# Sparse attention and a dense layer on one core: own keys, summaries and edge keys in one 128-row block

## The chip, the cores and the metric

The kernel runs on one core of a Trainium2 chip. The core has TensorE (matrix products, PE in the profile; its weight loads are PEld), VectorE (DVE), ScalarE (ACT), GpSimd (POOL) and SyncE (SP), with an on-chip memory of 128 partitions (SBUF) and a smaller accumulator memory (PSUM, eight banks of 2 KB per partition) that TensorE writes. DMA queues bring data from memory. The metric is the device time of one execution in microseconds.

## The reference

Two layers. The first is attention with 4 batches, 8 heads, 768 positions and 64 dimensions. Each query sees the keys less than 16 positions away, and one summary for each of 24 blocks of 32 keys: the maximum of the block's keys as key, the mean of its values as value, with log 32 added to the score. The second is a dense layer, 512 to 2048 to 512, with the gate h * clip(h + 3, 0, 6) / 6 between.

```python
k_sum = k.reshape(B, H, nb, block, D).max(axis=3)
v_sum = v.reshape(B, H, nb, block, D).mean(axis=3)
scores_l = scale * np.matmul(q, k.transpose(0, 1, 3, 2))
mask_l = np.abs(pos[:, None] - pos[None, :]) < window
scores_s = scale * np.einsum('bhsd,bhnd->bhsn', q, k_sum) + np.log(block)
scores_all = np.concatenate([np.where(mask_l, scores_l, -1e9), scores_s], axis=-1)
a = softmax(scores_all)
attn = np.matmul(a, np.concatenate([v, v_sum], axis=2))
x = attn.transpose(0, 2, 1, 3).reshape(B * S, H * D)
h = x @ w_in
out = (h * np.clip(h + 3.0, 0.0, 6.0) / 6.0) @ w_out
```

## The kernel before

Heads are taken in pairs p = 0 to 3, so that two heads of 64 dimensions fill 128 partitions. For each batch b and pair p:

- Tk (L264) transposes k by TensorE into PSUM. Copies put the two heads into `kbd[p]`, block-diagonal by blocks of 64 keys (L281, L283). A reduction takes the maximum of each 32 keys (L285, L287), and a product puts it into `kst[p]` (L292, L296). Tq (L298) transposes q and one copy puts it into `qT[p]`.
- Sl (L316) makes local scores by key blocks: for each block of 64 keys of both heads a matmul against the 94 queries in reach (L321), then the exponential (L324) and the product with a band mask (L325), into `at[p]`. Ss (L327) makes summary scores for two pairs at once, 96 rows, with an exponential of its own (L334) into `asum`.
- AV (L348) makes, for half of the positions, the numerator: one matmul of the summaries with `vst` (L357) and seven of local blocks with `vbd` (L359), added up in one bank; and the denominator by five matmuls with ones (L363 to L373). 1/den comes from a logarithm and an exponential (L375, L376), and x = num/den is written by VectorE (L377).

v comes twice: as blocks into `vbd` (block-diagonal, by load_v, or for batch 0 as float32 by load_vf and casts) and as rows (load_vrows) for the sums over 32 values, which vsum (L229) makes by six additions on VectorE; for batch 0 they come from TensorE (vsum0, L247).

The dense layer runs over eight stages t of 384 positions (two per batch). F1(t, ft) makes 128 of 2048 hidden columns: four matmuls (L389), the relu on ScalarE (L392), the gate product g on VectorE (L393). F2 adds 48 matmuls into three banks for three output tiles (L402); ScalarE copies each (L406) and SP stores it (L408).

The order. All engines run their instructions in program order, each its own list. Up to line 448 the order of TensorE, ScalarE and VectorE is written by hand: batch 0's attention for the first half of its positions. After it a work list of ten rows of 16 steps interleaves F1(t) with F2(t-1): first F1(0) alone, then F1(1) with F2(0), F2(1) alone, F1(2) alone, and from there F1(t) with F2(t-1). The attention of the batches is put at numbered steps ("slots", 16 to a row) between them, and a scheduler then settles each engine's order. GpSimd's order is the program's: it issues all loads, on one queue, and with hold_loads (L488) it waits for a gate product of step 11 before the loads of batch 1. Loads of later batches are placed at slots too, where their buffers are free.

Of the kernel before, what the change touches and what calls it, by code (L numbers as in the profile page):

```python
# [9 lines left out]
F32 = mybir.dt.float32  # L10
# [6 lines left out]
D = 64  # L17
BLK = 32
KB = 64
HALO = 15  # L20
WIN = KB + 2 * HALO
HALF = 384
NLONG = 2
RUN = 8
PCS = 4
RP = 96
QCUT = 480
# [3 lines left out]
def kernel(  # L31
# [13 lines left out]
    NT = S // 128  # L45
    NK = S // KB
# [8 lines left out]
    ld = ctx.enter_context(tc.tile_pool(name="ld", bufs=4))  # L55
    work = ctx.enter_context(tc.tile_pool(name="work", bufs=2))
    xp = ctx.enter_context(tc.tile_pool(name="xp", bufs=4))
# [11 lines left out]
    kbd = [const.tile([128, NK, 128], BF16, tag=f"kbd{p}", name=f"kbd{p}") for p in range(NP)]  # L69
    vall = const.tile([128, NP, NK, 128], BF16, tag="vbd", name="vbd")  # L70
    vbd = [vall[:, p] for p in range(NP)]
    qT = [const.tile([128, S + 2 * HALO + 2], BF16, tag=f"qT{p}", name=f"qT{p}") for p in range(NP)]
    at = [const.tile([128, NK, WIN], BF16, tag=f"at{p}", name=f"at{p}") for p in range(NP)]
    kst = [const.tile([128, RS], BF16, tag=f"kst{p}", name=f"kst{p}") for p in range(NP)]
    vst = [const.tile([RS, 2, D], BF16, tag=f"vst{p}", name=f"vst{p}") for p in range(NP)]
    w_in_sb = const.tile([128, NP, d_ff], BF16, tag="win", name="win")
    w_out_sb = const.tile([128, NFT, d_model], BF16, tag="wout", name="wout")


    kb_t, qb_t, vr_t, vf = {}, {}, {}, {}  # L80

    def load_k(b, p, n=1):

        if b < NLONG:
            t = ld.tile([RP, 2 * n, RUN, D], BF16, tag=f"kb{n}", name="kb", bufs=2)
            nc.gpsimd.dma_start(out=t[:], in_=k[b, 2 * p:2 * p + 2 * n].rearrange("h (p s) d -> p h s d", s=RUN))
        else:
            t = ld.tile([128, NT, 2, D], BF16, tag="kb", name="kb")
            load_natural(t, k, b, p)
        for i in range(n):  # L90
            kb_t[b, p + i] = t, i

    def load_q(b, p, n=1, part=None):

        if b < NLONG:
            lo, hi, r = cut(part)
            t = ld.tile([(hi - lo) // r, 2 * n, r, D], BF16, tag=f"qb{n}", name="qb", bufs=1 if n == 4 else 2)
            nc.gpsimd.dma_start(
                out=t[:], in_=q[b, 2 * p:2 * p + 2 * n, lo:hi].rearrange("h (p s) d -> p h s d", s=r))
        else:  # L100
            t = ld.tile([128, NT, 2, D], BF16, tag="qb", name="qb")
            load_natural(t, q, b, p)
        for i in range(n):
            qb_t[b, p + i, part] = t, i

    def cut(part):
        return {None: (0, S, RUN), 0: (0, QCUT, RUN // 2), 1: (QCUT, S, RUN // 2)}[part]

    def load_natural(t, src, b, p):
        for j in range(2):  # L110
            nc.gpsimd.dma_start(out=t[:, :, j], in_=src[b, 2 * p + j].rearrange("(s p) d -> p s d", p=128))  # L111

    def load_v(b, g, lo=0, hi=NK):

        for p in (2 * g, 2 * g + 1):
            for j in range(2):
                rows = slice(64 * j, 64 * j + 64)
                nc.gpsimd.dma_start(out=vall[rows, p, lo:hi, rows],  # L118
                                    in_=v[b, 2 * p + j].rearrange("(n k) d -> k n d", k=KB)[:, lo:hi])

    def load_vf(p):

        if not vf:
            t = gp.tile([128, NP, NK, D], F32, tag="g", name="vf")
            vf.update({i: t[:, i] for i in range(NP)})
        for j in range(2):
            nc.gpsimd.dma_start(out=vf[p][64 * j:64 * j + 64],  # L127
                                in_=v[0, 2 * p + j].rearrange("(n k) d -> k n d", k=KB))

    def load_vrows(b, g):  # L130

        w = BLK // PCS * D
        vr_t[b, g] = ld.tile([RS, PCS, w + 8], F32, tag="vr", name="vr", bufs=2)
        nc.gpsimd.dma_start(out=vr_t[b, g][:, :, 0:w],
                            in_=v[b, 4 * g:4 * g + 4].rearrange("h (n c t) d -> (h n) c (t d)", c=PCS, n=NB))
# [11 lines left out]


    ctx.enter_context(tc.manual_schedule(engines={ET.Pool}))
    start = tc.manual_schedule(engines={ET.PE, ET.Activation, ET.DVE})  # L150
    start.__enter__()
    load_vf(0)
# [4 lines left out]
    load_vf(1)  # L157
    load_k(0, 0)
    load_q(0, 0, 1, 0)
    load_vf(2)  # L160


    mask = const.tile([128, WIN], BF16, tag="mask", name="mask")
    nc.gpsimd.memset(mask[:], 1.0)
    for j in range(2):
        m = mask[j * 64:(j + 1) * 64]
        nc.gpsimd.affine_select(out=m, in_=m, compare_op=ALU.is_ge, fill=0.0, base=0,
                                channel_multiplier=-1, pattern=[[1, WIN]])
        nc.gpsimd.affine_select(out=m, in_=m, compare_op=ALU.is_ge, fill=0.0, base=2 * HALO,
                                channel_multiplier=1, pattern=[[-1, WIN]])  # L170
    load_vf(3)
    load_k(0, 1)
    load_q(0, 1, 1, 0)
    load_k(0, 2, 2)
    load_q(0, 2, 2, 0)


    hm4 = const.tile([RS, 4, D], F32, tag="hm4", name="hm4")
    osum4 = const.tile([RS, 4, D], BF16, tag="osum4", name="osum4")
    nc.gpsimd.memset(hm4[:], 1.0)  # L180
    nc.gpsimd.affine_select(out=hm4[:], in_=hm4[:], compare_op=ALU.is_ge, fill=0.0, base=0,
                            channel_multiplier=1, pattern=[[-NB, 4], [0, D]])
    nc.gpsimd.affine_select(out=hm4[:], in_=hm4[:], compare_op=ALU.is_ge, fill=0.0, base=NB - 1,
                            channel_multiplier=-1, pattern=[[NB, 4], [0, D]])
    hmv = [hm4[:, 2 * par:2 * par + 2] for par in range(2)]
    osum = [osum4[:, 2 * par:2 * par + 2] for par in range(2)]
    obd = const.tile([128, 2, D], BF16, tag="obd", name="obd")
    hmk = const.tile([128, 2, NB], BF16, tag="hmk", name="hmk")
    half_c = const.tile([128, 1], F32, tag="half", name="half_c")
    zero = const.tile([128, 1], F32, tag="zero", name="zero")  # L190
    nc.vector.memset(zero[:], 0.0)

    def zero_off_diagonal(eng, t):
        w = t.rearrange("p n c -> p (n c)").bitcast(F32).rearrange("p (n c) -> p n c", c=64)
        for r, c in ((slice(0, 64), slice(32, 64)), (slice(64, 128), slice(0, 32))):
            if eng is nc.scalar:
                eng.copy(w[r, :, c], zero[r].unsqueeze(2).to_broadcast([64, NK, 32]))
            else:
                eng.memset(w[r, :, c], 0.0)


    ind = const.tile([128, 2, 2, 4], F32, tag="ind", name="ind")
    nc.vector.memset(ind[:], 0.0)
    for i in range(4):
        for par in range(2):
            nc.vector.memset(ind[32 * i:32 * i + 32, par, par, i:i + 1], 1.0)
    for p in range(NP):
        zero_off_diagonal(nc.vector if p < 2 else nc.scalar, kbd[p][:])
# [336 lines left out]
```

## Time and profile before

| | us |
|---|---|
| Median of 3 runs | 265.46 |
| Lowest and highest | 264.72, 266.41 |
| The profiled execution's own span | 262.8 |
| TensorE busy (1848 matmuls) | 238.0 |
| ScalarE busy | 169.3 |
| VectorE busy | 154.2 |
| GpSimd busy (104 instructions) | 72.5 |
| F1 matmuls L389 (512) | 104.1 |
| F2 matmuls L402 (360 of 384 recorded) | 96.2 |

The span runs from the first to the last instruction of one execution. Matmuls overlap in the records, each being listed with the time until its end, so the cost of a run of them is read from the start of one to the start of the next. The page gives busy shares in 40 slices of the span, a chain of waits followed back from the end, and the costliest groups of instructions. The DMA row is the busy share of 16 DMA engines in tenths, and GB/s counts the bytes that are written; weights, q and k are read as float32 and written as bfloat16.

### The profile page before, as it was taken

To read this page: it belongs to the slowest core of one execution; us is meant where nothing else is said; L and a number is where in the kernel's file an instruction comes from. 1 tells how busy PE (TensorE), PEld (TensorE's weight loads), DVE (VectorE), ACT (ScalarE), POOL (GpSimd) and SP (SyncE) were. 2 spreads that over 40 slices of the span, in tenths; PEclk is the share of its full clock that TensorE was granted. 3 is DMA by queue.
4 is the path that set the end of the run, shared out by engine and by line. 5 is a ranking of instruction groups with operands and counts; after the bars stand their busy time and mean duration, and the time that the engine had idled before them with its cause. 6 is when DMAs were issued, how large, how long until landed. Compare 5 with 4: busy or idle time off the path is not lost.

```text
span 262.8 us, 4842 instructions
## 1 busy us (share of the span) xinstructions
PE 238.0 (91%) x1848; PEld 135.9 (52%) x1872; DVE 154.2 (59%) x360; ACT 169.3 (64%) x327; POOL 72.5 (28%) x104
## 2 busy tenths in 40 slices
PE   0946899999899969999899999999999999999993
PEld 0215556644455636666455556566655555555541
DVE  3594556632889774998994566668534544444400
ACT  7665578842587867998586567757766555555410
POOL 8994000566273600796920310000000000000000
PEclk9995599999999999999999999999999999999999
DMA  3999994299999971899990551001011111101122
GB/s 111 178 155 201 206 206 76 37 204 209 203 255 118 180 80 44 58 130 187 185 145 19 54 70 44 36 7 40 2 40 40 42 40 40 40 2 41 40 82 80
DMA packets 57848, 25.80 MB, mean 98 GB/s; under 512 B 45281, under 2 KB 53217, under 8 KB 57825
## 3 DMA queue, kind: packets, MB, share of 16 engines
q0 software_dynamic: 54160, 19.14, 63.5%
q1 hardware_dynamic: 3664, 6.34, 6.5%
q8 instruction: 15, 0.25, 0.4%
q14 instruction: 9, 0.07, 0.1%
HBM read 31.98 MB, written 6.29 MB: 146 GB/s over the span
## 4 chain that ended last, share of the span: by engine, by line
PE 62%; DMA 11%; DVE 8%; ACT 7%; POOL 7%; issue 3%; ACTq 0%; POOLq 0%
PE op L402 24%; PE hp L389 24%; DMA vr<-in_v_dram 8%; POOL vbd L118 3%; PE num L359 2%; DMA vs<-vs 2%; PE sl L321 2%; POOL vf L127 2%; DVE g L393 2%; PE num L357 2%; PE ss L331 2%; ACT kbd L281 2%; PE den L363 1%; PE den L366 1%; DMA vf<-in_v_dram 1%
## 5 line engine op out<-in xcount | busy, mean ns | idle before, releaser
L389 PE MATMUL hp<-x,win 128*128 128x384 bf16 x512 | 104.1, 326 | 2.8 <-DVE g L393 2.4
L392 ACT ACTIVATE r<-hp,half_c 128x384 f32<-128x384 f32 x128 | 73.5, 580 | 45.8 <-PE hp L389 45.0
L402 PE MATMUL op<-wout,g 128*128 128x512 bf16 x360 | 96.2, 379 | 1.1 <-issue 0.2
L393 DVE SCALAR_TENSOR_TENSOR g<-r,hp 128x384 bf16<-128x384 f32 x128 | 69.6, 551 | 45.6 <-ACT r L392 45.4
L389 PEld LDWEIGHTS <-win 128*128 128x128 bf16 x512 | 47.3, 98 | 37.2 <-issue 6.0
L402 PEld LDWEIGHTS <-g 128*128 128x128 bf16 x384 | 36.8, 98 | 32.8 <-issue 0.5
L377 DVE TENSOR_TENSOR x<-num,lg 128x384 bf16<-128x384 f32 x32 | 17.7, 555 | 24.7 <-ACT lg L376 22.8
L118 POOL DMA_DIRECT2D vbd<-in_v_dram x24 | 18.2, 775 | 37.7 <-PE num L359 33.6
L375 ACT ACTIVATE lg<-den 128x384 f32<-128x384 f32 x32 | 15.7, 492 | 16.0 <-PE den L373 7.4
L324 ACT ACTIVATE at<-sl 128x376 bf16<-128x376 f32 (+2 forms) x48 | 22.4, 490 | 2.3 <-PE sl L321 2.3
L406 ACT COPY ot<-op 128x512 f32<-128x512 f32 x24 | 13.9, 583 | 8.9 <-PE op L402 8.8
L325 DVE TENSOR_TENSOR at<-at,mask 128x376 bf16<-128x376 bf16 (+2 forms) x48 | 16.2, 349 | 3.6 <-ACT at L324 3.4
L359 PEld LDWEIGHTS <-vbd 128*128 128x128 bf16 x224 | 13.8, 102 | 8.0 <-issue 4.5
L376 ACT ACTIVATE lg<-lg 128x384 f32<-128x384 f32 x32 | 16.8, 526 | 0.8
L321 PE MATMUL sl<-qT,kbd 128*128 128x94 bf16 x192 | 15.0, 214 | 1.9 <-ACT at L324 0.8
L321 PEld LDWEIGHTS <-kbd 128*128 128x128 bf16 x192 | 12.2, 102 | 7.7 <-issue 1.8
L359 PE MATMUL num<-at,vbd 128*128 128x94 bf16 (+2 forms) x224 | 15.0, 206 | 0.0
L111 POOL DMA_DIRECT2D qb<-in_q_dram x16 | 13.5, 861 | 4.8 <-DMA vr<-in_v_dram 4.8
L252 PE MATMUL vps<-vf,ind 128*8 128x384 f32 x16 | 7.5, 612 | 7.6 <-DMA vf<-in_v_dram 7.6
L111 POOL DMA_DIRECT2D kb<-in_k_dram x16 | 13.5, 865 | 0.0
L357 PE MATMUL num<-asum,vst 96*128 96x384 bf16 x32 | 11.0, 344 | 2.6 <-DVE x L377 2.2
L281 ACT COPY kbd<-tp 64x768 bf16<-64x768 bf16 x12 | 9.5, 792 | 5.2 <-PE tp L271 5.1
(82 smaller groups left out, 219.8 us busy)
## 6 DMA issues: line engine op xcount, KB each, us to landing
out_dram<-ot SPq DMA_DIRECT2D x24, 256.0 KB, 2.0
vr<-in_v_dram POOLq DMA_DIRECT2D x6, 768.0 KB, 7.7
vbd<-in_v_dram POOLq DMA_DIRECT2D x24, 96.0 KB, 3.9
win<-in_moe_w_in_dram POOLq DMA_DIRECT2D x4, 512.0 KB, 11.1
wout<-in_moe_w_out_dram POOLq DMA_DIRECT2D x4, 512.0 KB, 18.3
vf<-in_v_dram POOLq DMA_DIRECT2D x8, 192.0 KB, 3.7
kb<-in_k_dram POOLq DMA_DIRECT2D x16, 96.0 KB, 6.8
qb<-in_q_dram POOLq DMA_DIRECT2D x16, 96.0 KB, 6.4
```

What stands on the lines that cost most here:

```text
L111: nc.gpsimd.dma_start(out=t[:, :, j], in_=src[b, 2 * p + j].rearrange("(s p) d -> p s d", p=128))
L118: nc.gpsimd.dma_start(out=vall[rows, p, lo:hi, rows], in_=v[b, 2 * p + j].rearrange("(n k) d -> k n d", k=KB)[:, lo:hi])
L321: nc.tensor.matmul(sp[:, i * WIN:(i + 1) * WIN], kbd[p][:, t], qT[p][:, t * KB:t * KB + WIN], start=True, stop=True)
L324: nc.scalar.activation(a, sp[:, 0:n * WIN].rearrange("p (n c) -> p n c", c=WIN), AF.Exp, scale=scl)
L357: nc.tensor.matmul(num[:], vst[p][:].rearrange("p h d -> p (h d)"), asm[:], start=True, stop=False)
L359: nc.tensor.matmul(num[:, lo:hi], vbd[p][:, t], a[:, t, off:off + hi - lo], start=False, stop=(i == len(bl) - 1))
L376: nc.scalar.activation(lg[:], lg[:], AF.Exp, scale=-1.0)
L377: nc.vector.tensor_tensor(xt[s][:, p], num[:], lg[:], op=ALU.mult)
L389: nc.tensor.matmul(hp[:], w_in_sb[:, kt, ft * 128:(ft + 1) * 128], xt[t][:, kt], start=(kt == 0), stop=(kt == NP - 1))
L392: nc.scalar.activation(r[:], hp[:], AF.Relu, bias=half_c[:], scale=1.0 / 6.0)
L393: nc.vector.scalar_tensor_tensor(gt[t][:, ft], r[:], 1.0, hp[:], op0=ALU.min, op1=ALU.mult)
L402: nc.tensor.matmul(op[:], gt[t][:, ft, ts * 128:(ts + 1) * 128], w_out_sb[:, ft], start=(ft == 0), stop=(ft == NFT - 1))
```

## The change

The attention goes over query blocks instead of key blocks. For each 64 queries, the 128 rows of the array hold: their own 64 keys (rows 0 to 63), the 24 summaries (64 to 87, and 8 rows of zeros), the last 16 keys of the block before (96 to 111) and the first 16 of the block after (112 to 127). q becomes block-diagonal, `qx[p]` with zeros for the other head, so that one matmul of 128 columns (64 queries of each head) makes all scores of a block. One exponential and one mask product follow. v is stored per block in the same row order, `va`, two buffers for even and odd batches; the middle of its three 64-column fields is zero, so that a 128-column window gives either head's weights.

```diff
+    kx = [const.tile([128, NQ, 128], BF16, tag=f"kx{p}", name=f"kx{p}") for p in range(NP)]
+    qx = [const.tile([128, NQ, 2, QB], BF16, tag=f"qx{p}", name=f"qx{p}") for p in range(NP)]
+    at = [const.tile([128, NQ, 2, QB], BF16, tag=f"at{p}", name=f"at{p}") for p in range(NP)]
+    va = [const.tile([128, NP, NQ, 3, D], BF16, tag=f"va{i}", name=f"va{i}") for i in range(2)]
...
+    def load_v(b, h):
+        o = va[b % 2][:, h // 2, :, 2 * (h % 2)]
+        own, tail, head = v_pieces(v[b, h])
+        nc.gpsimd.dma_start(out=o[0:QB], in_=own)
+        nc.gpsimd.dma_start(out=o[R_PREV:R_NEXT, 1:], in_=tail[:, 0:NQ - 1])
+        nc.gpsimd.dma_start(out=o[R_NEXT:128, 0:NQ - 1], in_=head[:, 1:])
...
+        (nc.gpsimd if b else nc.sync).dma_start(out=t[:], in_=v[b, 4 * g:4 * g + 4].rearrange("h (n t) d -> (h n) t d", n=NB))
...
+    def vsum(b, g):
+        vs = vs32[g] if b == 0 else work.tile([RS, D], F32, tag="vs", name="vs")
+        nc.vector.tensor_reduce(vs[0:RS], vr_t[b, g][:].rearrange("p t d -> p d t"), axis=AX.X, op=ALU.add)
+        if b:
+            nc.vector.tensor_copy(vst[g][0:RS], vs[:])
+        for i in range(4):
+            h = 4 * g + i
+            src = (vst[g] if b else vs32[g])[i * NB:i * NB + 32].unsqueeze(1).to_broadcast([32, NQ, D])
+            o = va[b % 2][:, h // 2, :, 2 * (h % 2)] if b else vf_t[g][:, i]
+            nc.sync.dma_start(out=o[R_SUM:R_PREV], in_=src)
...
+    def Tk(b, p):
...
+        nc.scalar.copy(kx[p][:, :, 0:QB].rearrange("p t (c s) -> p t c s", s=RUN),
+                       tp[:].rearrange("p (s t c) -> p t c s", s=RUN, t=NQ))
+        nc.vector.tensor_copy(kx[p][:, 1:, R_PREV:R_NEXT], kx[p][:, 0:NQ - 1, QB - EDGE:QB])
+        nc.vector.tensor_copy(kx[p][:, 0:NQ - 1, R_NEXT:], kx[p][:, 1:, 0:EDGE])
+        nc.vector.tensor_reduce(red[:], tp[:].rearrange("p (s n c) -> p n s c", s=RUN, n=NB), axis=AX.XY, op=ALU.max)
+        nc.vector.tensor_copy(kx[p][:, :, R_SUM:R_SUM + NB], red[:].unsqueeze(1).to_broadcast([128, NQ, NB]))
...
+    def Sc(b, p, lo, hi):
...
+            nc.tensor.matmul(sp[:, i], kx[p][:, t], qx[p][:, t], start=True, stop=True)
...
+        for i in range(NH):
+            t = half * NH + i
+            w = va[b % 2][:, p, t].rearrange("p j d -> p (j d)")
+            for j in range(2):
+                nc.tensor.matmul(num[:, i * QB:(i + 1) * QB], w[:, j * D:j * D + 128], a[:, t, j],
+                                 start=(i == 0 and j == 0), stop=(i == NH - 1 and j == 1))
...
+        for j in range(2):
+            nc.tensor.matmul(den[:].rearrange("p (t c) -> p t c", c=QB), w[:, j * D:j * D + 128],
+                             a[:, half * NH:(half + 1) * NH, j], start=(j == 0), stop=(j == 1))
...
-    at_slot(11, lambda: hold_loads(0, 11))
...
+    at_slot(11.5, lambda: loads(1))
+    at_slot(24, lambda: loads(2))
+    at_slot(60, lambda: loads(3))
```

The counts that follow: numerator matmuls 32 x 12 of 64 columns (before 32 x 8), denominator 32 x 2 (before 32 x 5), score matmuls 192 of 128 columns (before 192 of 94 and 32 of 384). All batches now load k and q in runs of eight positions and transpose them by sixteen matmuls of 96 columns, as batches 0 and 1 did; batches 2 and 3 had six of 128. The second head's q copy is VectorE's in every batch. The sums over v rows are one reduction of 96 x 2048 on VectorE, in place of six additions, and for batch 0 in place of the sums on TensorE. The sums then go by DMA, on SP, from SBUF to the summary rows of every block. Batch 0's v rows are loaded on SP at the very start; its float32 v blocks and their edges (load_vf, for four heads at a time) follow k and q on GpSimd's queue, then w_in, then the second half of q, then w_out. The order of GpSimd's loads after that is v rows, k and q, v blocks and edges of batch 1, and so on; hold_loads is gone, so a load waits for its buffer and for a free place among those under way. vsum of a batch is placed at the first slots of its attention, where it stood behind the transposes before. The buffers of x are three instead of four.

## The prediction, on record before the changed kernel ran

> **What bounds the kernel now.** I read the page first: busy shares, the rows of 40 slices, the chain of waits. Then the waits, the timeline of TensorE around each gap, and the DMA view of the start.
>
> ```profile
> span 262.8 us, 4842 instructions
> ...
> PE   0946899999899969999899999999999999999993
> ...
> PEclk9995599999999999999999999999999999999999
> DMA  3999994299999971899990551001011111101122
> GB/s 111 178 155 201 206 206 76 37 204 209 203 255 118 180 80 44 58 130 187 185 145 19 54 70 44 36 7 40 2 40 40 42 40 40 40 2 41 40 82 80
> ```
>
> A slice is 6.57 us. From slice 7 (39 us) on, TensorE is at 9 nearly everywhere: the bulk is bound by TensorE, and an edit there is worth what it takes from TensorE or from its few gaps. The first six slices differ: the DMA row is full and TensorE waits. The start ends when the loads of batch 0 and the weights have come in. The page's chain of waits says the same in shares:
>
> ```profile
> PE 62%; DMA 11%; DVE 8%; ACT 7%; POOL 7%; issue 3%; ACTq 0%; POOLq 0%
> ```
>
> The waits, taken from 60 us to the end for TensorE, show how little idle time is left behind the start:
>
> ```profile
> PE hp L389 <- DVE g L393: 2.2, 2, 1.2
> PE num L357 <- DVE x L377: 2.2, 1, 2.2
> ```
>
> The timeline shows the first of these: VectorE stood still for a load, and the dense layer's TensorE work behind it waited (the bracket is idle time and what ended it).
>
> ```profile
> 66.63 0.69 DVE L231 TENSOR_TENSOR vr<-vr 96x512 f32<-96x512 f32 x1 [2.59 <-DMA vr<-in_v_dram]
> ...
> 67.83 0.81 PE L389 MATMUL hp<-x,win 128*128 128x384 bf16 x4 [1.07 <-DVE g L393]
> ```
>
> This is the mechanism that decides my forecast: VectorE runs in program order, the sum over v rows waits for its load there, and the gate products (g) behind it hold the PSUM banks that TensorE needs.
>
> **What TensorE saves.** The timeline of one AV of the old kernel, with the start of the next work at 105.32 (columns: start, us, instruction, count):
>
> ```profile
> 104.47 0.33 PE L357 MATMUL num<-asum,vst 96*128 96x384 bf16 x1
> 104.63 0.44 PE L359 MATMUL num<-at,vbd 128*128 128x15 bf16 x7
> 104.91 0.33 PE L363 MATMUL den<-asum,osum 96*128 96x384 bf16 x1
> 105.08 0.33 PE L366 MATMUL den<-at,obd 128*128 128x384 bf16 x1
> 105.25 0.20 PE L372 MATMUL den<-at,obd 128*128 128x75 bf16 x1
> 105.28 0.20 PE L373 MATMUL den<-at,obd 128*128 128x90 bf16 x1
> 105.32 1.46 PE L389 MATMUL hp<-x,win 128*128 128x384 bf16 x8
> ```
>
> Matmuls overlap, so I cost them from start to start. An AV takes 0.85 us. The new one has 12 matmuls of 64 columns and two of 384. Eight 94-column matmuls (L321) took 0.33 us from 107.04 to 107.37, 41 ns each; a 64-column one lies between 28 ns (by columns) and 41 ns (if loading weights sets the pace). With 0.165 us for each 384, an AV costs 0.67 to 0.82; I take 0.70, by columns, since the seven of L359 with their mean of 78 columns took 40 ns each: 0.15 saved. For scores, a pair of heads paid 12 x 41 ns plus two L331 at 0.165, 0.82 us; now 12 of 128 columns, 56 ns by columns, 0.67: again 0.15. Transposes get dearer in batches 2 and 3: six 128-column ones took 0.33 us (121.92 to 122.25), sixteen of 96 took 0.46 (65.92 to 66.38), so 0.13 more, 16 times. Behind the start: 24 AVs x 0.15 = 3.6, 12 pairs x 0.15 = 1.8, less 2.1: **3.3 us saved**. The bounds are 0.5 and 4.2.
>
> **VectorE and ScalarE.** Per pair and batch VectorE drops kst (0.18), one k copy (0.56 or 0.96), the q copy (0.55) and half of the add tree (six adds and two products, 3.5 us a group: 1.8 per pair). It gains the strided q copy of one head (0.96, as L281), two edge copies and a spread copy (0.18 to 0.3 each, between the 48-element L296 at 0.18 and the 282-element mask product at 0.30), larger mask products (0.43 by the slope of L325 from 376 to 470, 56 ns in 94, instead of 0.35), and the one reduction that replaces the tree. That reduces 96x2048; the row of L285 is 954 ns for 768, so 2.5 us by element. Sum about even. ScalarE drops the two summary exps of a group (0.49 each) and pays 0.60 for an exp of 512 instead of 0.49, and copies 128 partitions instead of 64 for the same 0.79: with the second q copy some 0.5 us more per pair in batches 2 and 3. ScalarE is at 65% there, and TensorE's work hides it; between 110 and 120 us it stood at 9.2 of 10 us, so up to 2 us may show. I take **+0.5**.
>
> **The loads at the start, which decide.** The DMA row is full until the weights are in, so what stands ahead in the queue sets the times. Before: v 1536 KB, k and q 768 each, weights 4096, 7.4 MB by 43.5 us. After, by shapes in the diff: v rows for batch 0 (1536 KB, new, on SP), k 768, q 768, v blocks 1536, the 16-row edges 4 x 188 = 752 (new), the summary copies on SP, 8 x 96 = 768 (new), the weights 4096; then v rows of batch 1, first group, 768. No wait on a gate product (L490) holds that last load any more, but it still stands behind w_out. Rates: 206 GB/s in the slices with weights alone; 178 and 155 in those with v, k and q, I take 170; 255 in the slice with v rows. So 4.19 MB / 206 = 20.4 us, 1.57 / 255 = 6.2, the 4.7 MB of small pieces / 170 = 27.7, and 0.79 / 255 = 3.1: 57.4 us, and with the first packets at 2.7 us the load lands at **60 us**. Bounds: all at 230 GB/s gives 52, all at 169 (the mean of the DMA view over the first 44 us) gives 69.
>
> The page "DMA: Bandwidth & Descriptors" of the Trainium skill (section "Anatomy of one DMA") has 2 us and bytes / 436 GB/s for such a transfer; by that the 11.3 MB would be in by 31 us and the stall below would vanish. The weights' slices, at 206 GB/s of what is written, speak against it.
>
> Who waits: the transposes of the second half of q (Tq(0,p,1)) stand in TensorE's order behind the first four F1 steps, and q's second half is now behind all of w_in; the same rates without w_out and the last load make it 47 us, where the old one ran at 38.4. The larger wait is VectorE's. In the changed program its order has six gate products of the first F1 stage, then the reduction of batch 1's v rows, then the seventh. From 47 us on those six with their copies and masks take some 5 us, so VectorE gets there near 52 us and stands until 60. TensorE fills the PSUM banks up to the eighth F1 step and stops. From 60 us VectorE works off: the reduction 2.5, ten gate products at 0.55, two x at 0.56, two q copies at 0.5, four mask products 1.4, the second group's reduction 2.5 and its cast 0.15, some 1 us waiting for an AV between: 15.2. The second accumulator of F2 takes the bank that the last of these gate products frees, so F2 runs freely from about 75.3. In the old timeline it did from 54.8 (six L402 in a row). **+20.5 us.**
>
> TensorE idles twice for more than 5 us. After the old idle gap of 3.6 us (PE tp L271 <- DMA kb) the clock in the slices stood at 5 for 13 us. Some 8 us of TensorE work (eight F1 steps at 0.65, three AVs, the last scores) are due within the 15 us above; at half clock for all of them 16, so 0 to 4 us more; I take **+1**.
>
> The page "TensorE: Matmul & The Clock Gate" (part 1) has full clock back after about 3.4 us of sustained work; by that this term is 0.
>
> What comes back: the 1.07 us above and the like one near 126 us, where VectorE again waited for v rows; loads of later batches now run early, so **-2**. Output stores on SP now queue behind summary copies that wait for a reduction; three output buffers and a whole F2 stage lie between, so nothing.
>
> The summary transfer of the old start (the chain has it at 6.2 us) and the old sums on TensorE go, but they end before 30 us, where the loads now end later: nothing.
>
> Sum: 262.8 + 20.5 + 1 + 0.5 - 3.3 - 2 = 279.5 for the span. The runs' median of 265.46 is 2.7 over the profiled span, so **282 us**.
>
> **Rivals.**
> - *The queue drains fast enough* (this ends on the other side). SP's and GpSimd's queues side by side might raise the rate; the 255 slice shows more than 206 is possible. From 238 GB/s on for everything, v rows land by 50 us, q's half by 38, and nothing stalls: 265.5 - 3.3 - 2 = 260. Against it: the first slices held 155 to 178 on the very pieces that the change adds to. 6%. In between, near 230 GB/s, the stall costs what TensorE saves, 263 to 268: 5%.
> - *A slower queue.* The 256-byte pieces (edges, summary copies) may run below the 155 slice; all at 169 or less on average gives 69 us, 9 more: 290 to 291. 15%.
> - *SP's order bites.* The stores of F2 wait behind batch 3's summary copies, these behind a load; ScalarE's output copy then blocks, and the gate's relu behind it. Decides once a summary is later than three stores; some 5 us, 287. 4%.
>
> **How the numbers follow.** The forecast has 70% with 275 to 288 as its own range (v rows landing at 53 to 66). Low end 269: a landing at 52 and the full saving, 282 - 8 - 1, less 4 for both queues side by side; high end 291: the slow queue. Against a bound of 1%, which a measurement here can tell: faster 0.06, same 0.05, slower 0.89.
>
> **What would show it.** Right: a VectorE wait of 5 to 12 us on a DMA of v rows in the reduction, near 50 us, with TensorE idle in the same slices; F2 starting at 70 to 78 us; DMA full until about 63 us; from 80 us on a span 4 to 6 us shorter than before. Wrong: v rows landing before 52 us, F2 starting before 62, or gaps of TensorE behind 80 us that sum to over 10 us.

## The result and the profile after

| | before | after |
|---|---|---|
| Median, us | 265.88 (4 runs) | 291.15 (4 runs, 290.48 to 292.19) |
| Ratio, 95% interval | | 1.0947 (1.09 to 1.0995) |
| Span of the profiled execution | 262.8 | 289.1 |
| First F1 matmul starts at | 34.85 | 51.92 |
| First F2 matmul starts at | 52.59 | 78.34 |
| From there to the last matmul's start | 205.80 | 206.44 |
| TensorE busy / VectorE busy | 238.0 / 154.2 | 230.5 / 179.6 |

The kernel became 9.5% slower, 291.15 us against a forecast of 282, and just outside the stated range of 269 to 291. The table says where the 26.3 us of span come from: F1 starts 17.1 us later, F1's first stage takes 8.7 more (26.4 instead of 17.7), and everything behind, where I expected a gain, is longer by 0.6. The page of the kernel after:

```profile
span 289.1 us, 5297 instructions
...
PE   0123232694989997799997899999999999999994
...
PEclk9999999996999999999999999999999999999999
DMA  7999999999999999996999220010100100100111
GB/s 187 191 108 185 132 196 201 209 234 204 115 126 206 231 164 117 144 246 114 135 74 65 64 64 12 28 39 36 41 2 36 39 36 36 39 36 36 40 73 73
...
PE 49%; DMA 22%; DVE 11%; ACT 7%; issue 7%; POOL 3%; DVEq 0%; ACTq 0%; POOLq 0%
```

A slice is 7.23 us. In front TensorE has seven slices of 3 tenths or less; before there was one. The DMA row is full, yet the bytes are not those of a full queue: slices 3 and 5 of the GB/s row (14 to 22 us and 29 to 36 us) moved 108 and 132 against 206 with weights alone. In the chain of waits DMA has doubled its share.

Why F1 starts late is read from the casts of batch 0's v (L326, VectorE and ScalarE by turns). First their timeline on VectorE, then on ScalarE, then SP's issues of batch 0's summary copies, and their row in the list of DMA issues (KB each, us from issue to landing):

```profile
37.66 0.96 DVE L326 CAST va<-vf 128x1536 bf16<-128x1536 f32 x1 [5.05 <-DMA vf<-vs]
47.80 0.96 DVE L326 CAST va<-vf 128x1536 bf16<-128x1536 f32 x1 [5.17 <-DMA vf<-vs]
```

```profile
26.30 1.47 ACT L326 CAST va<-vf 128x1536 bf16<-128x1536 f32 x1 [3.10 <-DMA vf<-vs]
```

```profile
10.25 22.58 SPq L129 DMA_DIRECT2D vf<-vs  x8
```

```profile
vf<-vs SPq DMA_DIRECT2D x8, 96.0 KB, 22.8
```

A cast needs all 128 rows of a v block, the summary rows among them. These come by eight copies of 96 KB, each in 384 pieces of 256 bytes. SP needed 22.58 us to get them issued, in the median they landed 22.8 us after their issue, and the last cast ended at 48.8 us. AV and F1 follow from there. In VectorE's order each cast also stands in front of the next pair's k copies and q copy, so that the wait of one pair is passed on to TensorE's next scores.

Then F1's first stage. VectorE, and TensorE beside it:

```profile
65.03 3.57 DVE L122 TENSOR_REDUCE vs<-vr 96x64 f32<-96x2048 f32 x1 [1.38 <-DMA vr<-in_v_dram]
...
77.39 3.65 DVE L122 TENSOR_REDUCE vs<-vr 96x64 f32<-96x2048 f32 x1
```

```profile
57.36 0.36 PE L249 MATMUL tpq<-ident,qb 96*64 96x96 bf16 x8 [2.11 <-DVE g L307]
69.12 1.44 PE L303 MATMUL hp<-x,win 128*128 128x384 bf16 x4 [4.76 <-DVE g L307]
81.55 0.59 PE L315 MATMUL op<-wout,g 128*128 128x512 bf16 x2 [1.33 <-DVE g L307]
```

Batch 1's v rows landed at 65 us, so VectorE waited for them only 1.4 us: it had come late itself. But the reduction takes 3.6 us, twice, with gate products behind it each time, and in front of the first gate product twelve small memsets (zero_va of the second va tile, 53.83 to 56.75) had cost TensorE the gap at 57 us.

Behind 83 us four gaps of TensorE of over 1 us remain, each behind one reduction of a later batch. TensorE's, and VectorE's reductions in the same stretch:

```profile
114.83 0.38 PE L263 MATMUL sp<-qx,kx 128*128 128x128 bf16 x4 [1.47 <-DVE qx L255]
122.02 0.62 PE L263 MATMUL sp<-qx,kx 128*128 128x128 bf16 x8 [1.56 <-DVE qx L255]
158.25 0.81 PE L303 MATMUL hp<-x,win 128*128 128x384 bf16 x4 [1.68 <-DVE g L307]
165.27 1.46 PE L303 MATMUL hp<-x,win 128*128 128x384 bf16 x8 [1.42 <-DVE g L307]
```

```profile
110.13 3.65 DVE L122 TENSOR_REDUCE vs<-vr 96x64 f32<-96x2048 f32 x1
117.31 3.67 DVE L122 TENSOR_REDUCE vs<-vr 96x64 f32<-96x2048 f32 x1
154.10 3.64 DVE L122 TENSOR_REDUCE vs<-vr 96x64 f32<-96x2048 f32 x1
160.29 3.66 DVE L122 TENSOR_REDUCE vs<-vr 96x64 f32<-96x2048 f32 x1
```

TensorE goes on for about 2 of the 3.65 us in which VectorE is held, no longer.

The theory I set out to test: (1) batch 0's small summary copies set F1's start; (2) batch 1's v rows and their two reductions then stand in front of the gate products, a second delay behind the first; (3) the undivided reductions take back what TensorE saves later. The rival for (1) was my forecast's own picture, bytes in a full queue; for (3), that VectorE simply has 25 us more to do.

### The profile page after: what moved, and what is told of

It reads as the page before. It is cut to its first block, busy times and chain, and to the rows that moved or that the text cites. A ratio compares the mean times of both kernels' runs of the same rounds, so it can differ in the third digit from the quotient of the medians.

```text
span 289.1 us, 5297 instructions
## 1 busy us (share of the span) xinstructions
PE 230.5 (80%) x2048; PEld 132.4 (46%) x2048; DVE 179.6 (62%) x362; ACT 165.1 (57%) x307; POOL 76.0 (26%) x130
## 4 chain that ended last, share of the span: by engine, by line
PE 49%; DMA 22%; DVE 11%; ACT 7%; issue 7%; POOL 3%; DVEq 0%; ACTq 0%; POOLq 0%
PE op L315 23%; PE hp L303 20%; DMA vr<-in_v_dram 7%; DMA win<-in_moe_w_in_dram 7%; DMA vf<-in_v_dram 4%; DMA va<-in_v_dram 3%; DVE vs L122 3%; ACT r L306 2%; PE num L283 2%; DVE red L238 2%; DVE qx L255 2%; ACT kx L233 2%; DVE g L307 2%; PE den L288 1%; PE sp L263 1%
## 5 line engine op out<-in xcount | busy, mean ns | idle before, releaser
L265 ACT ACTIVATE at<-sp 128x512 bf16<-128x512 f32 (+1 forms) x52 | 27.9, 566 | 23.8 <-PE sp L263 23.7
L263 PE MATMUL sp<-qx,kx 128*128 128x128 bf16 x192 | 18.3, 232 | 23.1 <-DVE qx L255 22.4
L122 DVE TENSOR_REDUCE vs<-vr 96x64 f32<-96x2048 f32 x8 | 29.0, 3628 | 1.4 <-DMA vr<-in_v_dram 1.4
L263 PEld LDWEIGHTS <-kx 128*128 128x128 bf16 x192 | 14.6, 104 | 30.5 <-issue 23.9
L293 DVE TENSOR_TENSOR x<-num,lg 128x384 bf16<-128x384 f32 x32 | 17.7, 555 | 16.3 <-ACT lg L292 16.1
L267 DVE TENSOR_TENSOR at<-at,mask 128x512 bf16<-128x512 bf16 (+1 forms) x52 | 19.9, 400 | 9.3 <-ACT at L265 8.9
L283 PE MATMUL num<-at,va 128*128 128x64 bf16 x384 | 18.3, 199 | 5.7 <-DVE x L293 5.5
L283 PEld LDWEIGHTS <-va 128*128 128x128 bf16 x384 | 16.6, 102 | 12.0 <-issue 7.3
L99 POOL DMA_DIRECT2D va<-in_v_dram x24 | 18.9, 787 | 6.5 <-DMA vr<-in_v_dram 2.9
L233 ACT COPY kx<-tpk 128x768 bf16<-128x768 bf16 x16 | 13.0, 810 | 11.0 <-PE tpk L232 10.7
L288 PE MATMUL den<-at,ones 128*128 128x384 bf16 x64 | 17.2, 350 | 0.1
L255 DVE COPY qx<-tpq 64x768 bf16<-64x768 bf16 (+1 forms) x20 | 16.0, 801 | 0.9
## 6 DMA issues: line engine op xcount, KB each, us to landing
qb<-in_q_dram POOLq DMA_DIRECT2D x7, 384.0 KB, 12.8
```

The source lines that it names most:

```text
L99: nc.gpsimd.dma_start(out=o[0:QB], in_=own)
L122: nc.vector.tensor_reduce(vs[0:RS], vr_t[b, g][:].rearrange("p t d -> p d t"), axis=AX.X, op=ALU.add)
L255: copy(qx[p][rows, t0:t0 + nt, j].rearrange("p t (c s) -> p t c s", s=r), tp[rows, 0:n].rearrange("p (s t c) -> p t c s", s=r, t=nt))
L263: nc.tensor.matmul(sp[:, i], kx[p][:, t], qx[p][:, t], start=True, stop=True)
L265: nc.scalar.activation(a, sp[:, 0:n], AF.Exp, scale=scl)
L267: nc.vector.tensor_tensor(a, a, mask[:, m0:m0 + n].unsqueeze(2).to_broadcast([128, n, 2, QB]), op=ALU.mult)
```

## The experiments

Times are medians; the kernel before ran beside each set at 265.85 to 266.88 us. "First F1" and "first F2" are starts of the first matmul, read from the one profiled execution of each run. Most rows are two executions; after, e8, e9 and e13 are four, e11 six, e12 ten.

| run | us | ratio (95%) | first F1 | first F2 | first F2 to last matmul |
|---|---|---|---|---|---|
| after | 291.15 | 1.0947 (1.09 to 1.0995) | 51.92 | 78.34 | 206.44 |
| e1 no copies | 284.72 | 1.0679 (1.0594 to 1.0765) | 39.63 | 72.21 | 207.16 |
| e2 no rows of batch 1 | 282.45 | 1.0594 (1.0524 to 1.0665) | 51.32 | 71.29 | 205.57 |
| e3 no copies, wait back | 273.51 | 1.0259 (1.0204 to 1.0314) | 39.65 | 59.93 | 207.46 |
| e4 wait back | 284.39 | 1.0667 (1.0596 to 1.0738) | 51.12 | 71.04 | 207.75 |
| e5 wide copies | 289.02 | 1.0863 (1.0773 to 1.0952) | 44.51 | 77.31 | 206.53 |
| e6 sums in pieces | 278.35 | 1.0461 (1.0354 to 1.0569) | 52.73 | 74.31 | 199.30 |
| e7 wide, wait | 277.74 | 1.0438 (1.0355 to 1.0522) | 44.12 | 64.05 | 206.89 |
| e8 e7, pieces, zeroing | 270.39 | 1.0175 (1.0111 to 1.0238) | 43.87 | 61.23 | 201.74 |
| e9 sums on TensorE | 271.22 | 1.0186 (1.0104 to 1.0269) | 47.33 | 64.32 | 201.58 |
| e10 zeroing alone | 286.33 | 1.0761 (1.0643 to 1.0878) | 50.90 | 74.49 | 206.54 |
| e11 pairs overlapped | 268.65 | 1.0086 (1.0049 to 1.0123) | 41.95 | 63.12 | 200.35 |
| e12 e11, wait | 266.49 | 1.0017 (0.9986 to 1.0048) | 43.05 | 60.06 | 200.98 |
| e13 e12, weights last | 263.99 | 0.9887 (0.982 to 0.9953) | 36.77 | 57.32 | 200.94 |
| e14 weights after copies | 293.12 | 1.0977 (1.0888 to 1.1066) | 45.86 | 81.19 | 206.28 |

### The copies, the rows, and both (e1 to e4)

**e1**, batch 0's copies left out:

```diff
+            if b:
                 nc.sync.dma_start(out=o[R_SUM:R_PREV], in_=src)
```

> Leaves out batch 0's eight summary copies from SBUF to SBUF (its summary rows of v are zeros; batches 1 to 3 as they were). Theory A, the small copies share the DMA engines with the big loads packet by packet and land late, and the casts, the AVs and the first F1 step wait for them: F1 starts near 38 us instead of 51.9; VectorE then reaches batch 1's reduction early and its wait for v rows grows from 1.4 to 6 to 9 us, so F2 runs freely from 76 to 77 us instead of 83.4 and the span is about 282. Theory B, the queue is full of bytes and the copies count only by their 0.8 MB: F1 starts near 47, the wait stays near 1.4, the span is about 284.

**e2**, batch 1's row loads and reductions left out:

```diff
+        if b > 1:
             load_vrows(b, 0)
             load_vrows(b, 1)
```

> Leaves out batch 1's load of v rows and its two reductions (its summaries of v are those of batch 0). Theory A with its second part, that VectorE's two reductions of 3.6 us stand in front of the gate products of F1(0): the start of F1 stays at 51 to 52 us, the stage of F1(0) gets shorter by 1.4 + 7.3 us less what ran beside it, F2 runs freely from about 75, span about 281. Theory B: only the 1.4 us wait and 0.8 MB of the queue, span about 286.

**e3**, e1's edit with GpSimd's wait before batch 1's loads restored, and **e4**, that wait alone:

```diff
+    at_slot(11, lambda: hold_loads(0, 11))
     at_slot(11.5, lambda: loads(1))
```

> Both together: batch 0's summary copies left out (its summary rows of v are zeros), and the loads of batch 1 held back until the gate product of F1 step 11, as the old kernel held them, which also moves batch 1's reductions on VectorE behind the sixteen gate products of F1(0). Theory A: the two delays stand one behind the other, and without both F1 starts near 38 and F2 runs freely from 58 to 61 us, span 265 to 269, more than the two alone add up to. Theory B: about 5 us from the bytes and a few from the hold, span 277 to 282.

> The hold on batch 1's loads alone (as in the old kernel). Theory A: F1 starts at 51 to 52 as before, the reductions no longer stand in front of F1(0)'s gate products, F2 runs freely from 74 to 76 us, span 281 to 284, if the reductions then find room beside F1(1) and F2(0). Theory B: v rows land later still, and the span is 289 or more.

Without the copies F1 starts 12.3 us earlier, at 39.63; the picture of bytes had 47. Yet the whole gains only some 6 us, and VectorE's row in e1 shows where the other six stay:

```profile
58.77 3.57 DVE L122 TENSOR_REDUCE vs<-vr 96x64 f32<-96x2048 f32 x1 [7.36 <-DMA vr<-in_v_dram]
```

Its wait for batch 1's v rows has grown from 1.38 to 7.36 us. TensorE stands 10.7 us behind it. Taking the rows away alone (e2) gains 7.9 us of span, the restored wait alone (e4) 5.9, the copies alone 5.4; copies and wait together (e3) gain 17.3, not 11.3. That is what two delays in a row look like: each hides behind the other. With the wait, batch 1's rows are issued later (at 68.97 us in e4, in place of 43.47), and the first reduction comes only at 74.79, behind the first F2 matmul. e4 takes no bytes and no work away, so it is the place of the reduction that counts. F1's first stage falls from 26.4 us to 20.0 in e2 and 19.9 in e4. Points (1) and (2) stand. The other 4.8 us by which F1 starts later in e1 than in the kernel before are not separated by these runs. e3's span of 271.8 stayed above the 269 that I had allowed it; one gap behind an undivided reduction is still there (2.67 us, until 68.07).

### Bytes or pieces (e5, e14)

**e5** keeps the bytes of the copies and makes 3072-byte pieces of them:

```diff
+            nc.scalar.copy(vsb[0:RS + 8, g], vs32[g][:].unsqueeze(1).to_broadcast([RS + 8, NQ, D]))
...
+            src = vsb[i * NB:i * NB + 32, g] if b == 0 else ...
```

> Nothing is left out. Batch 0's eight summary copies carry the same 0.8 MB, but ScalarE first repeats each summary twelve times side by side in a helper tile (two operations of 768 columns, about 0.8 us each while ScalarE is idle), so a copy consists of 32 pieces of 3072 bytes in place of 384 of 256 bytes. Theory A (it is the number of small pieces that makes the copies late, since each takes its turn among the 1024-byte pieces of the weights): the copies land within some 6 us of their issue instead of 22.8, the casts no longer wait, F1 starts at 39 to 41 us, and as in the run without copies VectorE then waits 5 to 8 us more for batch 1's v rows; 284 to 286 us. Theory B (the same bytes through a full queue): copies land as late as before, F1 starts at 51 to 52, 290 to 292 us.

The copies are out of the way. SP's issues of all eight:

```profile
11.04 5.97 SPq L131 DMA_DIRECT2D vf<-vsb  x8
```

And their row in the list of DMA issues:

```profile
vf<-vsb SPq DMA_DIRECT2D x8, 96.0 KB, 12.5
```

5.97 us to issue instead of 22.58 for the same bytes, 12.5 us from issue to landing instead of 22.8 (theory A had 6), and of the casts only ScalarE's first waits, 0.8 us. But F1 starts at 44.5, not 39 to 41. TensorE waits for k there:

```profile
28.39 0.85 PE L236 MATMUL tpk<-ident,kb 96*64 96x96 bf16 x16 [4.56 <-DMA kb<-in_k_dram]
```

This k came 3.3 us earlier in the kernel after (25.08); that the small pieces left it more of the queue there fits, but isn't shown. So of e1's 12.3 us, 7.4 are due to the number of pieces. The other 4.9 go with the bytes and with the two copies of 0.83 us that e5 adds on ScalarE, which this run doesn't part. I had given all to the pieces. F2 gains hardly anything (77.31): the rows again. The total of 289.02 lies between the ranges of the two theories, and its interval overlaps that of the kernel after.

**e14** leaves the pieces small and keeps the weights back until the last copy has landed:

```diff
+    nc.gpsimd.tensor_copy(turn[R_SUM:R_PREV], vf_t[1][R_SUM:R_PREV, 3, 0, 0:2])
     for c in range(4):
         load_w_in(c)
```

> Nothing is left out. The changed kernel with one edit: GpSimd waits for the last of batch 0's eight summary copies before it issues the loads of the weights, so that the copies share the queue with k, q and v alone. Theory A (a piece of 256 bytes takes its turn among the 1024-byte pieces of the weights, and it is these turns that made the copies late): the last copy lands by 26 us in place of 32 or later, the casts' waits shrink from 5 us each to 2 or less, F1 starts at 42 to 47 us in place of 51.9; batch 1's v rows then wait as in the run without copies, so the whole gains 2 to 6 us: 285 to 289 us. Theory B (the copies are slow by themselves, 384 pieces each from one small queue, whatever else is in the queue): they land as late as before, the weights come later still, F1 starts at 53 to 58 us, 293 to 298 us.

F1's start, 45.86, went as theory A has it, the copies less so. SP's issues took 16.89 us instead of 22.58. The last copy landed at 37.2 us, when GpSimd's wait ended, and not by 26; the second cast still waited 3.38 us for one (at 35.76), and only the last two no longer waited. GpSimd's wait, and the copies' row in the list of DMA issues:

```profile
37.20 0.18 POOL L223 COPY turn<-vf 32x2 f32<-32x2 f32 x1 [21.84 <-DMA vf<-vs]
```

```profile
vf<-vs SPq DMA_DIRECT2D x8, 96.0 KB, 15.9
```

The total did not gain: 293.1, with an interval that overlaps that of the kernel after, because batch 1's v rows now came behind later weights:

```profile
67.12 3.57 DVE L122 TENSOR_REDUCE vs<-vr 96x64 f32<-96x2048 f32 x1 [7.01 <-DMA vr<-in_v_dram]
```

I had made the same mistake again and not carried the later weights through to the rows. On the open question the two measures differ. Of the 16.6 us that lie between small and wide pieces in SP's issue time, the weights explain 5.7; of the 10.3 us that lie between them from issue to landing (22.8, 15.9 and 12.5), they explain 6.9. So each theory has a part: the weights slow the copies, and copies in small pieces stay slower than wide ones when only k, q and v share the queue. Whether they would on an empty queue was not tried.

The Trainium skill says on "DMA: Bandwidth & Descriptors" (section "Queues, rings and completion order") that a DMA engine goes round its queues by whole packets; e14's shorter issue fits that. The same page (section "Why small descriptors are slow (HBM only)") has transfers within SBUF free of the penalty for small pieces. Here 22.58 against 5.97 us for the same bytes within SBUF speaks against relying on it while other queues are busy.

### The undivided reduction and the zeroing (e6, e10)

**e6** makes a sum by six additions from batch 1 on:

```diff
+            for lo, n, off in ((0, 8, 16), (8, 8, 16), (0, 8, 8), (0, 4, 4), (0, 2, 2)):
+                nc.vector.tensor_tensor(r[:, lo:lo + n], r[:, lo:lo + n], r[:, lo + off:lo + off + n], op=ALU.add)
+            nc.vector.tensor_tensor(vst[g][0:RS], r[:, 0], r[:, 1], op=ALU.add)
```

> Nothing is left out. From batch 1 on, a v sum is made by six additions on halves (512, 512, 512, 256, 128, 64 columns; 684, 684, 684, 417, 283 and 218 ns by the rows of the kernel before, 2.97 us together) in place of one reduction of 3.63 us. Theory A (it is the undivided 3.6 us in front of gate products and q copies that stops TensorE behind 80 us): the four TensorE gaps of 1.8 to 2.1 us at 113, 120, 156 and 163 us go, and the start gains 1 us: 284 to 287 us. Theory B (VectorE has too much to do in all, and its backlog stops TensorE however the work is cut): it gains no more than the 0.66 us of each sum that is in front of TensorE, 289 to 291 us.

It gained 12.8 us (11.1 of span; its two executions are 3.4 us apart), where I had 4 to 7. Part of VectorE's timeline in e6:

```profile
72.20 1.02 DVE L311 SCALAR_TENSOR_TENSOR g<-r,hp 128x384 bf16<-128x384 f32 x2
73.14 0.68 DVE L127 TENSOR_TENSOR vr<-vr 96x512 f32<-96x512 f32 x1
73.75 0.54 DVE L311 SCALAR_TENSOR_TENSOR g<-r,hp 128x384 bf16<-128x384 f32 x1
74.21 0.55 DVE L297 TENSOR_TENSOR x<-num,lg 128x384 bf16<-128x384 f32 x1
74.68 0.55 DVE L311 SCALAR_TENSOR_TENSOR g<-r,hp 128x384 bf16<-128x384 f32 x1
```

Pieces and gate products take turns. Of the 11.1 us of span, 7.1 lie behind the first F2 matmul (206.44 to 199.30), where VectorE's work fell by only 3.8 us in all (132.0 us busy to 128.2): point (3) holds, against the rival. Four come from in front of it, where I had counted one: F1's first stage is 4.8 us shorter, its TensorE gap of 4.76 us has shrunk to 1.75, and the mean granted clock of the stage is 1.00 instead of 0.87. The saving that I forecast for the steady part comes out once the sums are in pieces: from first F2 to the last matmul e6 is 6.5 us shorter than the kernel before.

"VectorE: DVE Perf Modes" of the Trainium skill (section "Rules for kernel authors") calls tensor_reduce, the operation used here, the slowest of the engine and advises to consider restructuring it on a hot path. The advice is borne out by these 12.8 us; most of them come from the pieces taking turns with gate products, for the work itself fell only from 3.63 to 2.97 us a sum.

**e10** moves the zeroing of the second va tile to the third pair of batch 0:

```diff
+        if p == 2:
+            zero_va(1)
```

> Nothing is left out. The changed kernel with only one edit: the zeroing of the second va tile (2.9 us of VectorE in front of F1's first gate product) moves to the third pair of batch 0. Theory A (batch 1's v rows land at 65 us and set when F2 starts; the zeroing is hidden behind them): the TensorE gap of 2.4 us at 55 us goes, VectorE waits so much longer for the rows, 289.5 to 291.5 us. Theory B (the zeroing is on the path to F2): 288 to 289 us.

286.33 us, better than either theory had it. The rows landed at 65.5, as before, but VectorE's order had changed: ten gate products now stood in front of the first reduction instead of six. So the landing of the rows limits only what stands behind the reduction, and a move of 2.9 us of work changes how much that is. My theory A had treated the landing as a wall for the whole stage.

### Putting the repairs together (e7, e8, e9, e11 to e13)

> Nothing is left out. Wide copies of the first run of this set, and GpSimd's wait before batch 1's loads put back. Theory A (two delays stand one behind the other, the copies and then batch 1's v rows, and either hides the other when it goes alone): as in the run with copies left out and the wait put back: F1 starts at 39 to 41 us, F2 is free at 62 to 65, 272 to 275 us. Theory B (that run gained because 0.8 MB were not carried): 280 to 284 us, as with the wait alone.

> Nothing is left out. The wide copies, GpSimd's wait, the sums in six pieces, and the zeroing of the second va tile moved from in front of F1's first gate product to the third pair of batch 0, where VectorE waits for data. Theory A (the four losses add up: copies, rows, undivided sums, zeroing): 273.5 of the run with the first two, less 4 to 6 for the undivided sums, less 2.4 for the zeroing: 264 to 268 us, level with the kernel before. Theory B (TensorE's gaps come back elsewhere because VectorE has 25 us more to do in all): 270 to 273 us.

e7 joins the edits of e4 and e5, e8 adds those of e6 and e10. 277.74 and 270.39, each some 2.5 us above A's range, e8 inside B's. But B's reason explains 2.4 us at most, the difference of the steady part to e6's (201.74 against 199.30): what is missing is mainly that F1 starts at 44, as in e5, where I had 39 to 41. From F1's start the stages are as short as expected: to the first F2 17.4 us in e8 against 17.7 before, and 4.1 less than before from there to the end.

**e9** starts from e8, makes batch 0's sums on TensorE from the cast blocks, and drops the rows, reductions and copies of batch 0:

```diff
-    load_vrows(0, 0)
-    load_vrows(0, 1)
...
+        for t in range(NQ):
+            nc.tensor.matmul(vs[:], ind[:, t], va[0][0:QB, p, t, 0:3:2], start=(t == 0), stop=(t == NQ - 1))
+        (nc.vector.tensor_copy if p % 2 else nc.scalar.copy)(
+            va[0][R_SUM:R_PREV, p, :, 0:3:2], vs[R_SUM:R_PREV].unsqueeze(1).to_broadcast([32, NQ, 2, D]))
```

> Nothing is left out. On top of the run with all four repairs, batch 0's summaries need no transfer at all: TensorE sums each pair's cast own rows (12 products of 128 columns with a 0/1 tile, per pair) into PSUM rows 64 to 95, and one copy per pair spreads them over the 12 blocks; the 1.57 MB of batch 0's v rows that SP loaded for the sums, the two reductions and the eight copies go. The casts are cut in two (own rows, edge rows). Theory A (F1's start is what the first transfers cost: with 0.8 MB of copies in wide pieces 43.9 us, without copies 39.6): another 1.57 MB less makes it 34 to 38 us, and 7 to 10 us come off the 270.4: 260 to 264 us, below the kernel before. Theory B (F1's start is now set by k and q blocks and the extra copies on ScalarE and VectorE, about 1 us each, eight more): F1 starts at 39 to 43 us, 265 to 270 us.

A fell, and B, right in kind, was not late enough: 2.4 MB less in the queue, and F1 starts at 47.3, the whole no faster than e8 (271.22 against 270.39). The chain of waits of e9 (start, us, what) shows engines where loads had been:

```profile
36.19 1.75 DVE va L336
37.98 0.96 DVE va L328
38.99 1.47 PE vs L335 x12
```

With the copies gone the start was a chain of VectorE, TensorE and ScalarE, one pair after the other, and my edit had put more links into it, the zeroing of e8 (2.8 us) among them.

**e11** and **e12** start from e9. GpSimd issues the k and q of the last two pairs before it builds the masks (in the kernel after, the first group's v blocks stand ahead of them in its order), it takes over the zeroing from VectorE, each pair's transposes go ahead of the scores of the pair before, and the casts are whole again. e12 keeps the wait before batch 1's loads, e11 doesn't.

```diff
+    for p in range(NP + 1):
+        if p < NP:
+            Tk(0, p)
+            Tq(0, p, 0)
+        if p:
+            Sc(0, p - 1, 0, 4)
+            Sc(0, p - 1, 4, 6)
```

> Nothing is left out. The run with sums on TensorE had F1 at 47.3 us although the queue had moved 2.4 MB less: behind the third pair's k (landed at 21.5) TensorE, ScalarE and VectorE passed one pair after the other through scores, casts and spreads. Here GpSimd issues the third and fourth pair's k and q before it builds the masks, each pair's transposes stand in front of the scores of the pair before, the casts are whole again (ScalarE fills the unloaded rows with zeros early), and GpSimd does the zeroing of the second va tile; there is no wait before batch 1's loads. Theory A (F1's start is now a chain of engines, which overlap shortens): k of the last pairs lands near 13 us, F1 starts at 31 to 36 us, batch 1's v rows land by 45: 256 to 263 us, below the kernel before. Theory B (the transfers set it: the weights of F1 land no earlier): F1 starts at 38 or later, 264 us or more.

> Nothing is left out. The run of this set without it, and GpSimd's wait for the 12th gate product before batch 1's loads. Theory A (with an early F1 the weights and batch 1's loads have room one behind the other, and the wait only delays batch 1's v rows, for whose sums VectorE then stands in front of F2): 2 to 6 us slower than the run without the wait. Theory B (the wait puts the weights ahead of the v rows in the queue, as it did in the kernel as changed, where it gained 5.9 us of span): up to 4 us faster.

268.65 and 266.49: e12 is level with the kernel before. In e11 and e12 F1 starts at 42 to 43, theory B's side, since v now comes late, issued by 14.5 us and landed at 31.9 (e12) among the weights. The wait gained 2.2 us, also on B's side: it leaves the order of the queue to the weights. Hence **e13**, e12 with the weights of F1 held until batch 0's v has landed:

```diff
+    nc.gpsimd.tensor_copy(turn[R_PREV:], vf_t[1][R_PREV:, 3, 1, 0:2])
     for c in range(4):
         load_w_in(c)
```

> Nothing is left out. The run with overlapped pairs and GpSimd's wait before batch 1's loads, and one more wait on GpSimd: the weights of F1 are issued only when batch 0's v loads have landed (there the second v load was issued at 14.5 us and landed at 31.9, among the weights). Theory A (turns): the v load lands by 25 us, the last cast and the sums follow, F1 starts at 36 to 40 us in place of 43.0, 260 to 264 us. Theory B (v in 256-byte pieces is slow by itself, the weights only fill what it leaves): the v load lands at 28 or later, the weights later by as much, F1 starts at 43 to 47 us, 267 to 271 us.

VectorE's casts in e12, and then in e13:

```profile
22.03 0.96 DVE L338 CAST va<-vf 128x1536 bf16<-128x1536 f32 x1 [3.90 <-DMA vf<-in_v_dram]
31.93 0.96 DVE L338 CAST va<-vf 128x1536 bf16<-128x1536 f32 x1 [4.75 <-DMA vf<-in_v_dram]
```

```profile
19.54 0.96 DVE L340 CAST va<-vf 128x1536 bf16<-128x1536 f32 x1 [1.42 <-DMA vf<-in_v_dram]
25.78 0.96 DVE L340 CAST va<-vf 128x1536 bf16<-128x1536 f32 x1 [1.08 <-DMA vf<-in_v_dram]
```

v lands 6 us earlier, F1 starts 6.3 us earlier, and 2.5 us of it reach the end, for q's second half comes later now (TensorE waits 2.55 us for it at 42.8): 263.99 us, ratio 0.9887 (0.982 to 0.9953) to the kernel before in its set, whose medians over all sets lie between 265.46 and 266.88. So the new attention can beat the old one by 1% or a little less, once its start is rebuilt. Loads issued behind do slow loads issued ahead, theory A in this place.

## Why the prediction was wrong, step by step

- **Direction and mechanism of the second delay: right.** VectorE, in program order, was held at batch 1's v rows, and F2 waited behind it. I had the rows landing at 60 (52 to 69); they landed at 65. e2 and e4 show this part to be worth 6 to 8 us alone. The sign I had named, a wait of 5 to 12 us, was only 1.38 us long, since VectorE came late by the first delay; it shows as 7.36 in e1.
- **The step that failed** is "The loads at the start, which decide". It counted the summary copies as 8 x 96 KB in the sum of bytes and asked only when the last load lands. It did not ask who waits for the copies themselves: the casts, and behind them AV and F1. F1's start moved by 17.1 us. That was no term of mine; the one figure I had near it, 47 us for q's second half, was later than F1's start as I imagined it. e1 shows 12.3 of the 17.1 to hang on the copies, e5 7.4 of these on their 256-byte pieces. My rival of a slower queue named these pieces, but as a lower mean rate, not as a wait of their own; its 290 to 291 come near the measured time by luck, for they needed the rows to land at 69.
- **Two terms where one was priced.** The 20.5 us to a free F2 were all put on the landing of the rows. Measured to the first F2 matmul, 25.75: 17.1 before F1 and 8.7 in its first stage. By the forecast's own mark, six F2 matmuls in a row, it is 28.6 (83.42 against 54.80), so the term was 8.1 too small, and what it held came by another road.
- **The reduction was under-sized**, 2.5 us by element from a bf16 row; it took 3.63, eight times. I had called VectorE's sum about even; it is busy 25.4 us more. The reductions' excess over 2.5 is 9 us of that; the q copies, 16.0 us instead of 4.4, are a larger part, since batches 0 and 1 had no q copy on VectorE that could be dropped.
- **The zeroing of the second va tile** was left out, 2.9 us of VectorE in front of the first gate product; e10 makes it 3.7 us of span, 4.8 of the medians.
- **What TensorE saves: right by itself, lost elsewhere.** An AV takes 0.67 us from start to start (221.33 to 222.00, forecast 0.70), four score matmuls 0.22 (203.18 to 203.40), so 0.66 a pair (forecast 0.67). Forecast behind the start was a net gain of 4.8 us. Measured from the first F2 matmul it is a loss of 0.6, measured from the forecast's mark to the end of the span a gain of 2.3 (208.0 to 205.7); e6 brings out 6.5. The undivided reductions took it. My list said gaps behind 80 us summing to over 10 us would show me wrong; they sum to 8.3, 6.1 of it in the four shown, and as a sign that bound was too wide.
- **The clock: right in kind, half the size.** Behind the gap of 4.76 us the granted clock was 0.50 from 69 to 72 us and 0.74 from 72 to 75. TensorE was busy 19.34 us in the stage, and 17.45 in e6 with the same 168 matmuls at 1.00: 1.9 us, inside my 0 to 4; I took 1. The 0 that I set beside it doesn't follow from the 3.4 us quoted there: up to half of them, 1.7 us, could be lost, as an estimate.
- **"DMA full until about 63 us" was no sign at all.** The row stays at 9, but for one slice of 6, until 159 us, because later loads follow without a hold.
- **What comes back, 2 us:** the two old stalls on v rows near 67 and 126 us are gone, but reductions made new ones.

Put together from the stages as measured, the span is 262.8 + 17.1 (F1's start) + 8.7 (first stage) + 0.6 (the rest), 289.2 against 289.1. This says where the time lies and shows no cause; the causes rest on e1 to e6 and e10.

## What to carry to other kernels

When a load, copy or sum is moved, ask first who waits for it and what stands behind that waiter in its engine's order; the sum of bytes comes after. Two delays in a row hide each other, so test them together as well as alone (here 5.4 and 5.9 us apart, 17.3 together). On an engine that feeds TensorE's banks, cut long operations into pieces (here of 0.2 to 0.7 us): the same sums in six pieces each were worth 12.8 us of 291.

## What the runs showed of the hardware

- Eight copies of 96 KB within SBUF took SP 22.58 us to issue in pieces of 256 bytes beside a full queue, 16.89 without the weights behind them, and 5.97 in pieces of 3072 bytes; from issue to landing the medians were 22.8, 15.9 and 12.5 us.
- Loads issued later take a share from loads issued earlier on the same queue: batch 0's v landed at 31.9 us with the weights behind it, by 25.8 without.
- The granted clock of a profile doesn't tell all: in the first 51.92 us of the kernel after it reads 1.00, yet an AV took 1.28 us there from start to start (41.35 to 42.63, behind a gap of 8.13 us), against 0.67 later.
- A float32 reduction of 96x2048 with the summed dimension strided took 3.63 us, 1.77 ns an element; a bf16 one of 128x768 takes 0.96 us, 1.25 ns.
